# New places for conversions, turns, zeros and one routing chain in a linear-attention and two-MLP kernel

## The chip, the cores and the metric

The kernel runs on one core of one Trainium2 chip. The metric is the device time of one execution in microseconds (us). The engines of a core work from queues of their own, each strictly in order: TensorE (PE; its weight loads are shown as PEld), VectorE (DVE), ScalarE (ACT), GpSimd (POOL) and SyncE (SP), which here issues nearly all DMAs. Matmul results go to PSUM banks and are read from there by VectorE and ScalarE.

## The reference

Three stages, all in float32:

1. Linear attention with decay: 4 batches, 8 heads, 768 steps, head size 48. Per step, `cur = (u*k_t) outer v_t`, `y_t = r_t (state + cur)`, `state = w*state + k_t outer v_t`. The result, regrouped, is `x` of 3072 tokens x 384.
2. An MLP: `h = x @ w_in` (384 x 2048), `g = relu(h)^2`, `x = g @ w_out` (2048 x 384).
3. A mixture of 8 experts with noisy top-2 routing: `noisy = x @ w_gate + log1p(exp(x @ w_noise)) * noise`; the two largest per token are chosen, their softmax gives two weights; each token's output is the weighted sum of `relu(x @ w1[e]) @ w2[e]` (384 x 1024, 1024 x 384) over its two experts.

## The kernel before

All large products are done in a split form: a value is rounded to a shorter float ("high", fp32r) and its remainder kept ("low"), and three matmuls (high x high, high x low, low x high) take the place of one. So each product of 128x128 by 512 columns is three matmuls, and each activation and each weight needs a conversion: ScalarE writes the high part, VectorE (or GpSimd) subtracts to get the low part.

**First part, blocks j = 0 to 5** of 512 tokens. Per block there are 16 steps f. Each step issues mm1(j,f) (nine matmuls into a `ph` bank, of which there are two), gsplit(j,f) (Relu and two Squares on ScalarE, the subtract `gl` on VectorE), then the pieces that were put at slot 2f, then mm2 of two steps earlier (nine matmuls), then the pieces of slot 2f+1. A piece's place is written as a number: `put(8.8, ...)` means slot 8, ordered within it by the fraction. The pieces are the attention of the next block (pre, p_tr, p_a, p_y and so on: CHUNKS), the routing of the block before (ROUTE), and in the last block the preparation of the first experts. The order of a queue is the order in which the code issues; nothing is reordered later.

Attention chunks beyond the eighth read r and k by strided loads on SyncE (`load_next`, L205 to L218) into one buffer each (`rp`), which VectorE turns (L385) and GpSimd scales (L387) for the matmuls of p_a (L414).

**Routing of a block** is a chain: r_row (matmuls with the gate weights), r_soft1 to r_soft3 (softplus, with an Exp and a Ln on ScalarE), r_top1, r_top2, r_sel (small VectorE operations on 128 x 4 x 8), r_rank (three small matmuls on TensorE, L651 to L655, which read `sel`, `pre` and `tot` of r_sel; then VectorE makes the slot numbers `si`), r_w1 and r_w2 (weights, with an Exp), and eight r_send: indirect DMAs on GpSimd that write the tokens' rows to the experts' places in a DRAM buffer `sent`. ROUTE has three tables: for block j=1, for j=2 to 4, and for j=5, which routes block 4.

**Second part, the experts.** An expert e is worked in two units: (e,0), 512 tokens, and (e,1), 308 tokens. A unit fetches its rows (`fetch`: four DMAs of G and two small ones of gt, on SyncE), turns them (`turn`, three per unit: VectorE transposes, ScalarE copies to the high part, VectorE subtracts), goes up (8 steps f with Relu `hh` on ScalarE and `hl` on VectorE) and down. (e,0) goes down in four tiles of 24 matmuls; (e,1) goes down transposed, in three tiles of 24 (`down_t`), each copied out as `yT`, and is turned back in the next unit (`back`). Results are scaled on ScalarE and added to `out` in DRAM by indirect DMAs on GpSimd. The order of units is (0,0), (1,0), (0,1), (1,1), (2,0), (2,1), ..., (6,0), (6,1), (7,1), (7,0).

Expert weights come in eight pieces per expert, four for the first layer (w0) and four for the second (w1): `load_e` on SyncE into three staging buffers `ws` (one in block 5), `conv_e` on ScalarE and VectorE. `conv_next` converts the next piece and issues the load three pieces ahead, which can only start when a staging buffer is free. `put(n, ...)` in a unit gives a place after the Relu of step n (n under 8) or in down step n-8; `fill` holds pieces that are spread evenly over the unit.

`out` is first cleared by zero_out (before: one DMA of 4,800 KB, at slot 2.6 of block 2), and `sent` by eight DMAs of 1,375 KB in block 1.

Of the kernel before, what the change touches and what calls it, by code (L numbers as in the profile page):

```python
# [8 lines left out]
F32 = mybir.dt.float32  # L9
F32R = mybir.dt.float32r  # L10
# [7 lines left out]
P = 128  # L18
# [56 lines left out]


ROUTE_LAST = (0.6, 0.6, 0.8, 1.81, 1.8, 1.81, 2.8, 2.81, 2.82, 3.3, 3.8, 4.8, 5.3, 5.81, 4.8, 5.8, 8.8, 7.82, 10.8,
# [3 lines left out]
FETCH, TOTALS = 13.9, 13.95  # L81
TURN_10 = (8.8, 9.8, 10.8)
TURN_01 = (8.8, 9.8, 10.8)
TURN_11 = (7.3, 7.8, 8.81, 8.82, 8.83, 9.8, 9.81)
TURN = (7.8, 8.8, 8.81)


@with_exitstack
def body(ctx, tc, r, k, v, w, u, w_in, w_out, w_gate, w_noise, noise, w1, w2, out):
    nc = tc.nc  # L90
    B, H, S, D = r.shape
    DM = H * D
    FF = w_in.shape[1]
    E, _, F2 = w1.shape
    NT = B * S
    KD = DM // P
# [3 lines left out]
    NCH = NT // P  # L100
# [19 lines left out]
    def pool(name, side="left", stack=ctx, **kw):  # L120
        return stack.enter_context(tc.tile_pool(name=name, bufs=1, side=side, reuse_waits="tile", **kw))

    consts = pool("consts")
    eb = pool("eb", side="right")
# [4 lines left out]
    C = {}  # L129
# [199 lines left out]
        nc.sync.dma_start(sent[e * CAP:e * CAP + LAST * P, :].rearrange("(q p) x -> p q x", p=P),  # L329
                            C["zero"][:, None, :].to_broadcast([P, LAST, XW]))  # L330

    def zero_out():
        zero = eb.tile([P, DM], F32, name="zero2", tag="s3", bufs=1)
        nc.vector.memset(zero, 0.0)
        nc.sync.dma_start(out.rearrange("(q p) d -> p q d", p=P),
                          zero[:, None, :].to_broadcast([P, NCH + 1, DM]))

    x1h, x1l = {}, {}
    A = {}
# [147 lines left out]
    def mm1(j, f):  # L487
        ph = PH[j, f] = bank("ph", 2)
        qi, fo = divmod(f, NF // NP)
        sl = slice(fo * P, (fo + 1) * P)  # L490
        n = 0
        for d in range(KD):
            for wt, xt in ((wih, x1h), (wih, x1l), (wil, x1h)):
                nc.tensor.matmul(ph, wt[qi][:, d, sl], xt[j][:, d, :], start=(n == 0), stop=(n == 3 * KD - 1))  # L494
                n += 1
# [24 lines left out]
    def finish(j):  # L520
        xo = XO.pop(j)
        X2[j] = eb.tile([P, KD, BLK], F32, name="x2T", tag="s6", bufs=2)
        for d in range(KD):
            (nc.vector.tensor_copy if d == 1 else nc.scalar.copy)(X2[j][:, d, :], xo[:, d, :])
# [165 lines left out]
    W, RW, X, GT, HT, YT, IDX = {}, {}, {}, {}, {}, {}, {}  # L690
# [12 lines left out]
    NW = 4  # L703
# [26 lines left out]
    def tokens(un):  # L730
        a0, a1 = UNITS[un]
        return sum(width(a) for a in range(a0, a1))
# [4 lines left out]
    def fetched(un):  # L737
        return -(-tokens(un) // 32) * 32
# [18 lines left out]
        early.append(nc.sync.dma_start(gt[:, 1, :, None], rows[:, :, XW - 1:]))  # L757
        GT[e, un] = gt

    def turn(e, un, c):  # L760
        pl = pools["f2" if un else "f1"]
        if c == 0:
            X[e, un] = X[e, un], *(pl.tile([P, KD, fetched(un)], F32R, name=f"x{h}{un}") for h in "hl")
        g, xh, xl = X[e, un]
        n = fetched(un) // 32
        xt = pl.tile([P, fetched(un)], F32, name=f"xt{un}")
        nc.vector.transpose(xt.rearrange("p (s i) -> p i s", i=n),
                            g[:, :, 32 * c:32 * c + 32])
        nc.scalar.activation(xh[:, c, :], xt, AF.Copy)
        nc.vector.tensor_tensor(xl[:, c, :], xt, xh[:, c, :].bitcast(F32), op=OP.subtract)  # L770
        if c == KD - 1:
            X[e, un] = xh, xl
            idx = IDX[e, un] = pl.tile([P, UNITS[un][1] - UNITS[un][0]], I32, name=f"id{un}", bufs=2)
            nc.vector.tensor_copy(idx, GT[e, un][:, 1, :])
# [213 lines left out]
    for j in range(NB):  # L988
        slots = [[] for _ in range(2 * NF)]

        def put(n, fn, *args):
            k = int(n)
            slots[k].append((n - k, len(slots[k]), lambda: fn(*args)))

        if j + 1 < NB:
            for i, at_ in enumerate(CHUNKS[min(j, 2)]):
                q = (j + 1) * TPB + i
                todo = [(pre, ()), (p_tr, "r"), (p_tr, "k"), (pre2, ()), (p_kv, ()), (p_a, ()), (p_y, (0,)), (p_y, (1,)),
                        (p_x, ())]
                for n, (fn, args) in zip(at_, todo):  # L1000
                    if q > TPB or fn not in (pre, p_tr):
                        put(n, fn, q, *args)
        if j == 0:
            put(0.6, conv_w3, 2)
            for n in range(AW, 2 * NP):
                for at_, fn in zip(CONV_AT[n - AW], (conv_w1, conv_w2, conv_w3)):
                    put(at_, fn, n)
            put(30.6, load_routing)
        if j == 1:
            for e in range(E):  # L1010
                put(e * 3 // 2 + 3.6, zeros, e)
        if j == 2:
            put(2.6, zero_out)
        if j:
            plan = [(r_row, i) for i in range(TPB)] + [(fn,) for fn in (r_soft1, r_soft2, r_soft3, r_top1, r_top2, r_sel, r_w1, r_rank, r_w2)]
            plan += [(r_send, *divmod(i, 2)) for i in range(2 * TPB)]
            for n, (fn, *args) in zip(ROUTE[0 if j == 1 else 1 if j < NB - 1 else 2], plan):
                put(n, fn, j - 1, *args)
            for i, n in enumerate(RESTS[0 if j == 1 else 1 if j < NB - 1 else 2]):
                put(n, r_rest, j - 1, i)  # L1020
        if j == NB - 1:
            put(4.8, f1_open)
            put(4.8, load_e, 0, 0)
            put(20.8, fetch, 0, 0)
            for n in range(NW):
                put(8.8 + 4 * n, conv_e, 0, n)
                if n + 1 < NW:
                    put(8.8 + 4 * n, load_e, 0, n + 1)
            for c in range(KD):
                put(24.8 + 2 * c, turn, 0, 0, c)  # L1030
            put(30.9, fetch, 1, 0)
        slots = [[p for *_, p in sorted(s, key=lambda x: x[:2])] for s in slots]
        for f in range(NF):
            mm1(j, f)
            gsplit(j, f)
            for p in slots[2 * f]:
                p()
            g = j * NF + f - LAG
            if g >= 0:
                mm2(*divmod(g, NF))  # L1040
                if f == LAG - 1:
                    finish(j - 1)
            for p in slots[2 * f + 1]:
                p()
# [10 lines left out]
    def conv_next(eng=None):  # L1055
        conv_e(*todo.pop(0), eng)
        if len(todo) >= AHEAD:
            load_e(*todo[AHEAD - 1])

    def prepare(e, un):  # L1060
        return [lambda c=c: turn(e, un, c) for c in range(KD)]
# [6 lines left out]
    for e, un in order:  # L1068
        n_up = UNITS[un][1] - UNITS[un][0]
        fill, late = [], {}  # L1070
# [11 lines left out]
        if (e, un) == (0, 0):  # L1082
            plan = [(fn, i) for fn in (r_rest, r_row) for i in range(TPB)] + [(fn,) for fn in (r_soft1, r_soft2, r_soft3, r_top1, r_top2, r_sel, r_table, r_w1, r_rank, r_w2)]
            plan += [(r_send, *divmod(i, 2)) for i in range(2 * TPB)]
            plan = [(n, lambda fn=fn, args=args: fn(NB - 1, *args)) for n, (fn, *args) in zip(ROUTE_LAST, plan)]
            plan += [(n, lambda i=i: conv_next(nc.gpsimd if i < SPLIT_POOL else nc.vector)) for i, n in enumerate(CONV_E)]
            plan += list(zip(TURN_10, prepare(1, 0)))
            plan += [(FETCH, lambda: fetch(0, 1)), (TOTALS, totals)]
            carry = [(n - N0, fn) for n, fn in plan if n >= N0]
            for n, fn in plan:  # L1090
                if n < N0:
                    put(n, fn)
        elif (e, un) == (1, 0):
            for n, fn in carry:
                put(n, fn)
            for n in range(NW):
                put(n + 0.8, conv_next)
            put(NW + 0.8, lambda: fetch(2, 0))
            for n, fn in zip(TURN_01, prepare(0, 1)):
                put(n, fn)  # L1100
            put(TURN_01[-1], lambda: fetch(1, 1))
        elif (e, un) == (0, 1):
            for n, fn in zip(TURN_11, prepare(1, 1) + [conv_next] * NW):
                put(n, fn)
        else:
            if e + 1 < E:
                fill += [lambda: fetch(e + 1, un)] + [conv_next] * NW
            if un == 0 and e + 1 < E:
                fill += prepare(e, 1)
            elif e + 1 < E:  # L1110
                if e + 1 == E - 1:
                    fill += prepare(e + 1, 0)
                for n, fn in zip(TURN, prepare(e + 1, int(e + 1 == E - 1))):
                    put(n, fn)
                if (e, un) == (1, 1):
                    put(TURN[-1], lambda: fetch(3, 0))
            else:
                fill += [lambda: None] * NW
# [65 lines left out]
```

## Time and profile before

| what | value |
|---|---|
| time, three runs | 990.04 us median (989.67 to 991.66) |
| profiled execution | 994.35 us, span of its instructions 992.6 us |
| TensorE busy | 951.0 us (96%), mean granted clock 0.981 |
| VectorE busy | 543.4 us (55%) |
| ScalarE busy | 436.7 us (44%) |
| GpSimd busy | 350.8 us (35%) |
| SyncE's DMA queue (q1) | 91.22 MB, 36.2% of 16 engines' span |
| chain that ended last | PE 76%, DVE 10%, DMA 5%, ACT 3% |

Busy shares are averages over the whole span; matmuls are pipelined and their ends are modelled, so start times tell more than busy time. The granted clock is TensorE's clock as a share of full speed: 1.00 is 2.4 GHz, 0.50 is 1.2 GHz. Times in rows count from the first instruction of the span. In a row of the timeline, "[3.62 <-DMA rp<-in_r]" means that the engine was idle for 3.62 us before it and that this DMA ended the wait. In time, block 2 begins near 220 us, block 5 near 468, the experts at 546, unit (1,1) near 633 and (6,1) near 904.

### The profile page before, as it was taken

The numbers are of one execution on the slowest core, as the hardware profiler recorded it, in microseconds if no ns is written. First come the engines' busy times: TensorE is split into PE (matmuls) and PEld (weight loads), VectorE is DVE, ScalarE is ACT, GpSimd is POOL, SyncE is SP. The second block draws the span as 40 slices with busy tenths as digits, with TensorE's granted clock in tenths as the row PEclk, the third lists the DMA queues.
The fourth block names the chain that finished last, engine by engine and source line by source line (L and its number), as shares of the span: only waits on it lengthen the run. The fifth ranks groups of instructions, "written<-read, shape, count | busy, mean of one in ns | idle before, by whom it ended". The sixth has DMA issues, their size and how long they took to land.

```text
span 992.6 us, 17606 instructions
## 1 busy us (share of the span) xinstructions
PE 951.0 (96%) x6816; PEld 819.2 (83%) x6816; DVE 543.4 (55%) x986; ACT 436.7 (44%) x797; POOL 350.8 (35%) x407
## 2 busy tenths in 40 slices
PE   7898999998999999999998999899999999999995
PEld 6676788777778878877886899889999898989985
DVE  6899956535755673582343663454545454544420
ACT  4666755333344444443653642243434444443320
POOL 5555552553563363454030262022121212222112
PEclk7999999999999999999999999899999999999998
DMA  7645359938333152231033477366645555554112
GB/s 171 158 148 148 115 145 295 256 99 271 74 111 79 45 129 77 60 72 67 1 96 80 132 166 144 86 122 135 123 94 127 102 112 114 114 115 70 20 20 35
DMA packets 193301, 112.35 MB, mean 113 GB/s; under 512 B 131728, under 2 KB 185776, under 8 KB 193200
## 3 DMA queue, kind: packets, MB, share of 16 engines
q1 hardware_dynamic: 181776, 91.22, 36.2%
q0 software_dynamic: 10624, 19.74, 10.9%
q8 instruction: 65, 1.06, 0.4%
q14 instruction: 36, 0.29, 0.1%
q10 hardware_dynamic: 800, 0.02, 0.0%
HBM read 74.83 MB, written 36.12 MB: 112 GB/s over the span
## 4 chain that ended last, share of the span: by engine, by line
PE 76%; DVE 10%; DMA 5%; ACT 3%; issue 2%; SPq 2%; POOL 1%; POOLq 0%; ACTq 0%; DVEq 0%
PE ph L793 18%; PE ph L494 15%; PE xo L517 15%; PE y L844 13%; PE y L876 3%; PE att L432 3%; PE ph L876 2%; PE att L414 2%; PE y L793 2%; PE att L550 2%; DVE t L271 1%; DVE t L270 1%; DVE gl L506 1%; DMA ws<-in_moe_w 1%; DMA stg<-in_moe_w_in 1%
## 5 line engine op out<-in xcount | busy, mean ns | idle before, releaser
L855 POOL DMA_INDIRECT out<-yt,id x56 | 87.2, 1556 | 321.5 <-ACT yt L853 291.9
L506 DVE TENSOR_TENSOR gl<-g,gh 128x512 fp32r<-128x512 f32 x96 | 83.1, 866 | 144.6 <-ACT gh L504 138.6
L830 DVE SCALAR_TENSOR_TENSOR hl<-ph,hh 128x512 fp32r<-128x512 f32 (+1 forms) x112 | 66.6, 598 | 123.2 <-ACT hh L829 123.0
L500 ACT ACTIVATE rt<-ph 128x512 f32<-128x512 f32 x96 | 57.2, 596 | 162.2 <-PE ph L494 151.5
L793 PE MATMUL ph<-xh,w0h 128*128 128x512 f32 (+1 forms) x336 | 120.4, 358 | 4.6 <-ACT yT L880 4.2
L494 PE MATMUL ph<-x1h,wih 128*128 128x512 f32 x288 | 118.3, 411 | 2.4 <-ACT rt L500 1.8
L793 PE MATMUL ph<-xh,w0l 128*128 128x512 f32 (+2 forms) x336 | 117.8, 351 | 0.0
L793 PE MATMUL ph<-xl,w0h 128*128 128x512 f32 (+2 forms) x336 | 117.5, 350 | 0.2 <-DVE xl L770 0.2
L517 PE MATMUL xo<-gh,woh 128*128 128x512 f32 x288 | 115.2, 400 | 2.0 <-ACT gh L504 2.0
L517 PE MATMUL xo<-gh,wol 128*128 128x512 f32 x288 | 112.4, 390 | 0.9 <-POOL wol L284 0.9
L494 PE MATMUL ph<-x1l,wih 128*128 128x512 f32 x288 | 113.2, 393 | 0.1
L494 PE MATMUL ph<-x1h,wil 128*128 128x512 f32 x288 | 113.1, 393 | 0.0
L517 PE MATMUL xo<-gl,woh 128*128 128x512 f32 x288 | 112.6, 391 | 0.5 <-DVE gl L506 0.5
L829 ACT ACTIVATE hh<-ph 128x512 fp32r<-128x512 f32 (+1 forms) x112 | 58.6, 524 | 82.9 <-PE ph L793 77.0
L844 PE MATMUL y<-w1h,hh 128*128 128x384 f32 x256 | 85.7, 335 | 0.0
L844 PE MATMUL y<-w1l,hh 128*128 128x384 f32 x256 | 85.6, 335 | 0.0
L844 PE MATMUL y<-w1h,hl 128*128 128x384 f32 x256 | 85.6, 334 | 0.0
L678 POOL DMA_INDIRECT sent<-row,si x48 | 50.4, 1050 | 70.2 <-DVE si L670 50.6
L793 PEld LDWEIGHTS ph<-xh,w0h 128*128 128x128 f32 x336 | 64.0, 190 | 12.0 <-ACT yT L880 4.4
L793 PEld LDWEIGHTS ph<-xh,w0l 128*128 128x128 f32 x336 | 64.0, 191 | 8.0
L793 PEld LDWEIGHTS ph<-xl,w0h 128*128 128x128 f32 x336 | 64.2, 191 | 7.3 <-DVE xl L770 0.5
L494 PEld LDWEIGHTS ph<-x1h,wih 128*128 128x128 f32 x288 | 54.3, 189 | 19.0 <-ACT rt L500 2.9
(209 smaller groups left out, 2072.6 us busy)
## 6 DMA issues: line engine op xcount, KB each, us to landing
ws<-in_moe_w SPq DMA_DIRECT2D x128, 96.0 KB
ws<-in_moe_w SPq DMA_DIRECT2D x32, 384.0 KB
sent<-zero SPq DMA_DIRECT2D x8, 1375.5 KB
G<-sent SPq DMA_DIRECT2D x36, 192.0 KB
stg<-in_moe_w_in SPq DMA_DIRECT2D x8, 768.0 KB
stg<-in_moe_w_out SPq DMA_DIRECT2D x8, 768.0 KB
out<-zero SPq DMA_DIRECT2D x1, 4800.0 KB
lv<-in_v SPq DMA_DIRECT2D x24, 192.0 KB
```

The lines of the kernel that those rows point to most:

```text
L432: nc.tensor.matmul(pb[32 * n:32 * n + 32, d, :], x, y, skip_group_check=True, **kw)
L494: nc.tensor.matmul(ph, wt[qi][:, d, sl], xt[j][:, d, :], start=(n == 0), stop=(n == 3 * KD - 1))
L500: nc.scalar.activation(rt, ph, AF.Relu)
L506: nc.vector.tensor_tensor(gl, g, gh.bitcast(F32), op=OP.subtract)
L517: nc.tensor.matmul(XO[j][:, d, :], wt[qi][:, fo, sl], gt, start=(f == 0 and n == 0), stop=(f == NF - 1 and n == 2))
L678: st = nc.gpsimd.indirect_dma_start(out=sent, in_=s["row"][:, i, :], in_offset=None, out_offset=bass.IndirectOffsetOnAxis(ap=s["si"][:, i, ...
L793: nc.tensor.matmul(ph[:, c], wt[:, d, sl], xt[:, d, c], start=(m == 0), stop=(m == 3 * KD - 1))
L829: nc.scalar.activation(hh[:, :n], ph, AF.Relu)
L830: nc.vector.scalar_tensor_tensor(hl[:, :n], ph, 0.0, hh[:, :n].bitcast(F32), op0=OP.max, op1=OP.subtract)
L844: nc.tensor.matmul(py, ht[:, sl], wt[:, fo, :], start=(m == 0), stop=(m == 3 * NF2 - 1))
L855: st = nc.gpsimd.indirect_dma_start(out=out, in_=yt, in_offset=None, compute_op=OP.add, out_offset=bass.IndirectOffsetOnAxis(ap=IDX[e, un] ...
L876: nc.tensor.matmul(py[d][:, c], wt[:, fo, sl], ht[:, c], start=(m == 0), stop=(m == 3 * NF2 - 1))
```

## The change

Five groups of edits, all of places in the order of issue; the arithmetic is the same.

- ROUTE's third table: from r_soft3 on, the routing of block 4 comes earlier in block 5 (r_rank from 16.12 to 10.9, the sends from places between 16.16 and 20.68 to places between 12.1 and 16.3).
- `fetch(0,0)` moves from slot 20.8 to 16.7 and `fetch(1,0)` from 30.9 to 27.9. The three turns of (0,0), which came whole at 24.8, 26.8 and 28.8, come in two halves each, the transpose at 21.8, 23.8, 25.8 and the copy and subtract a slot later.
- zero_out goes in five DMAs of 960 KB: three in block 3 (slots 8.7, 14.7, 26.7), two in block 4 (8.7, 14.7). The memset of its source tile comes with the first.
- In unit (0,1), two of the four conversions (first-layer pieces of expert 2) come after the Relus of steps 4 and 5, and the other two after the second and third turn, one each, in place of all four behind the turns. The turns come at 7.8, 8.8, 9.8 in place of 7.3, 7.8, 8.81.
- The three turns of (7,0), which were spread over the up of (6,1), come in the down of (6,0).

```diff
-         (4.22, 4.4, 5.4, 5.47, 5.64, 6.68, 8.57, 8.78, 11.541, 12.732, 12.94, 16.12, 15.66,
-          20.4, 18.2, 16.55, 16.16, 17.28, 17.12, 20.1, 20.68))
+         (4.22, 4.4, 5.4, 5.47, 5.64, 6.68, 7.8, 7.81, 8.7, 9.5, 9.6, 10.9, 10.6,
+          12.1, 12.7, 13.3, 13.9, 14.5, 15.1, 15.7, 16.3))
+CLEAR = {3: (8.7, 14.7, 26.7), 4: (8.7, 14.7)}
+FETCH_00 = 16.7
+TURN_00 = ((21.8, 22.8), (23.8, 24.8), (25.8, 26.8))
...
-TURN_11 = (7.3, 7.8, 8.81, 8.82, 8.83, 9.8, 9.81)
+CONV_2 = (4.8, 5.8, 8.81, 9.81)
+TURN_11 = (7.8, 8.8, 9.8)
 TURN = (7.8, 8.8, 8.81)
+TURN_LAST = (9.8, 10.8, 11.8)
...
-    def zero_out():
-        zero = eb.tile([P, DM], F32, name="zero2", tag="s3", bufs=1)
-        nc.vector.memset(zero, 0.0)
-        nc.sync.dma_start(out.rearrange("(q p) d -> p q d", p=P),
-                          zero[:, None, :].to_broadcast([P, NCH + 1, DM]))
+    def zero_out(i, n):
+        if i == 0:
+            C["zero2"] = eb.tile([P, DM], F32, name="zero2", tag="s3", bufs=1)
+            nc.vector.memset(C["zero2"], 0.0)
+        a, b = i * (NCH + 1) // n, (i + 1) * (NCH + 1) // n
+        nc.sync.dma_start(out[a * P:b * P, :].rearrange("(q p) d -> p q d", p=P),
+                          C["zero2"][:, None, :].to_broadcast([P, b - a, DM]))
...
-    def turn(e, un, c):
+    XT = {}
+
+    def turn(e, un, c, parts="ab"):
         pl = pools["f2" if un else "f1"]
-        if c == 0:
-            X[e, un] = X[e, un], *(pl.tile([P, KD, fetched(un)], F32R, name=f"x{h}{un}") for h in "hl")
+        if "a" in parts:
+            if c == 0:
+                X[e, un] = X[e, un], *(pl.tile([P, KD, fetched(un)], F32R, name=f"x{h}{un}") for h in "hl")
+            n = fetched(un) // 32
+            XT[e, un] = pl.tile([P, fetched(un)], F32, name=f"xt{un}")
+            nc.vector.transpose(XT[e, un].rearrange("p (s i) -> p i s", i=n),
+                                X[e, un][0][:, :, 32 * c:32 * c + 32])
+        if "b" not in parts:
+            return
         g, xh, xl = X[e, un]
-        n = fetched(un) // 32
-        xt = pl.tile([P, fetched(un)], F32, name=f"xt{un}")
-        nc.vector.transpose(xt.rearrange("p (s i) -> p i s", i=n),
-                            g[:, :, 32 * c:32 * c + 32])
+        xt = XT.pop((e, un))
         nc.scalar.activation(xh[:, c, :], xt, AF.Copy)
...
-        if j == 2:
-            put(2.6, zero_out)
+        for i, n in enumerate(CLEAR.get(j, ())):
+            put(n, zero_out, i + sum(len(c) for k, c in CLEAR.items() if k < j), sum(map(len, CLEAR.values())))
...
-            put(20.8, fetch, 0, 0)
+            put(FETCH_00, fetch, 0, 0)
...
-            for c in range(KD):
-                put(24.8 + 2 * c, turn, 0, 0, c)
-            put(30.9, fetch, 1, 0)
+            for c, at_ in enumerate(TURN_00):
+                for n, part in zip(at_, "ab"):
+                    put(n, turn, 0, 0, c, part)
+            put(27.9, fetch, 1, 0)
...
         elif (e, un) == (0, 1):
-            for n, fn in zip(TURN_11, prepare(1, 1) + [conv_next] * NW):
+            for n, fn in zip(CONV_2 + TURN_11, [conv_next] * NW + prepare(1, 1)):
                 put(n, fn)
...
             if un == 0 and e + 1 < E:
                 fill += prepare(e, 1)
+                if e + 1 == E - 1:
+                    for n, fn in zip(TURN_LAST, prepare(e + 1, 0)):
+                        put(n, fn)
             elif e + 1 < E:
-                if e + 1 == E - 1:
-                    fill += prepare(e + 1, 0)
                 for n, fn in zip(TURN, prepare(e + 1, int(e + 1 == E - 1))):
```

## Rows read from the trace of the kernel before

**Rows 1.** Windows: stretch, us; PE, PEld, DVE, ACT, POOL busy; PEclk, DMA, GB/s.
```profile
122.00:209.00 87.00, 87.00 (x685) 69.35 (x677) 50.44 (x108) 38.66 (x68) 44.91 (x52) 1.00 0.77 216
248.93:252.35 3.42, 3.42 (x9) 2.67 (x8) 2.41 (x3) 0.07 (x1) 3.17 (x3) 0.50 0.16 40
531.04:546.24 15.20, 11.67 (x46) 8.21 (x45) 7.24 (x10) 6.80 (x12) 0.00 (x0) 1.00 0.26 53
638.05:644.88 6.83, 6.09 (x24) 6.09 (x25) 1.34 (x2) 1.02 (x3) 0.00 (x0) 0.50 0.54 135
921.36:924.77 3.41, 3.41 (x15) 3.41 (x15) 2.45 (x5) 1.07 (x3) 0.00 (x0) 0.50 0.00 0
```

**Rows 2.** Whom TensorE waited for: us in total, times, longest; the span.
```profile
PE ph L793 <- ACT yT L880: 4.2, 1, 4.2
PE att L414 <- POOL kT L387: 3.1, 1, 3.1
...
PE y L876 <- ACT hh L829: 1.4, 1, 1.4
```

**Rows 3.** Timeline of TensorE in block 5: start, us, engine, line, operation.
```profile
494.11 0.39 PE L517 MATMUL xo<-gh,woh 128*128 128x512 f32 x1
...
496.15 0.39 PE L494 MATMUL ph<-x1h,wih 128*128 128x512 f32 x1
...
531.04 0.39 PE L517 MATMUL xo<-gh,woh 128*128 128x512 f32 x1
...
546.24 0.39 PE L793 MATMUL ph<-xh,w0h 128*128 128x512 f32 x1
```

**Rows 4.** Timeline of TensorE in unit (6,1).
```profile
904.19 0.30 PE L793 MATMUL ph<-xh,w0h 128*128 128x308 f32 x1
...
914.40 0.30 PE L876 MATMUL y<-hh,w1h 128*128 128x308 f32 x1
...
928.95 0.31 PE L793 MATMUL ph<-xh,w0h 128*128 128x308 f32 x1
```

**Rows 5.** Timeline of SyncE's queue: DMA issues of block 2, block 5 and (0,1).
```profile
224.28 8.21 SPq L537 DMA_DIRECT2D noise<-in_moe_noise  x1
...
525.39 2.71 SPq L752 DMA_DIRECT2D G<-sent  x4
...
632.30 1.75 SPq L717 DMA_DIRECT2D ws<-in_moe_w  x4
```

**Rows 6.** Timeline of VectorE in blocks 2 and 5.
```profile
242.80 1.09 DVE L385 STREAM_TRANSPOSE rT<-rp 128x512 f32<-128x512 f32 x1 [3.62 <-DMA rp<-in_r]
...
489.95 0.19 DVE L584 TENSOR_TENSOR d<-d,q 128x32 f32<-128x32 f32 x1
...
492.71 0.18 DVE L589 TENSOR_TENSOR ln<-ln,d 128x32 f32<-128x32 f32 x1
...
496.19 0.69 DVE L506 TENSOR_TENSOR gl<-g,gh 128x512 fp32r<-128x512 f32 x1 [0.23 <-ACT gh L504]
...
497.68 0.19 DVE L563 TENSOR_TENSOR oh<-oh,oh2m 128x32 f32<-128x32 f32 x1
...
500.87 0.18 DVE L613 TENSOR_TENSOR sel<-oh,oh 128x32 bf16<-128x32 f32 x1
...
501.71 0.17 DVE L619 TENSOR_TENSOR tot<-pre,sel 128x8 bf16<-128x8 bf16 x1
...
532.05 1.05 DVE L767 STREAM_TRANSPOSE xt<-G 128x512 f32<-128x512 f32 x1 [6.41 <-DMA G<-sent]
```

**Rows 7.** Timeline of GpSimd in block 5: the first send.
```profile
511.42 1.05 POOL L678 DMA_INDIRECT sent<-row,si  x1 [50.61 <-DVE si L670]
```

**Rows 8.** The chain that ended last, in time: start, us, what.
```profile
521.16 4.15 DMA sent<-row,si
...
633.62 3.82 DMA ws<-in_moe_w
```

**Rows 9.** Timeline of ScalarE in unit (0,1).
```profile
637.60 0.84 ACT L726 ACTIVATE w0h<-ws 128x768 fp32r<-128x768 f32 x1 [4.84 <-DMA ws<-in_moe_w]
```

## The prediction

> **What bounds the kernel now.** Read the list of what TensorE waited for first, then the granted clock in chosen stretches, then the start times of its matmuls around each wait. TensorE is the bound: in most stretches it is busy without a break, for instance all 87 us from 122 to 209 [rows 1]. So the kernel can only become faster where TensorE stands still, and each such place has a price of two parts, the wait and, behind some waits, a stretch at the lower of its two clock levels (0.50, 1.2 GHz), in which the same matmuls take twice as long. Leaving the start of the kernel aside, four places stand out, and the change touches each.
>
> 1. Block 2 (244 us): 3.1 us for kT [rows 2], then 3.42 us at 0.50 [rows 1], of which half is lost: 3.1 + 1.7 = 4.8 us.
> 2. End of block 5: one group of nine matmuls takes 496.15 - 494.11 = 2.04 us [rows 3]. From 531.04 to the first matmul of the experts at 546.24 lie five groups, mm2(12), mm1(15), mm2(13) to mm2(15): 15.2 us where 10.2 would do, so 5.0 us lost.
> 3. From the down of (0,1) into (1,1): 4.2 us for yT [rows 2], then 6.09 us of busy time at 0.50 [rows 1], half of it lost: 7.25 us.
> 4. Unit (6,1): its up, 72 matmuls of 308 columns, takes 914.40 - 904.19 = 10.21 us; its down, again 72 of 308, takes 928.95 - 914.40 = 14.55 us [rows 4], with a wait for hh [rows 2] and a half-clock stretch [rows 1] in it: 4.3 us lost.
>
> Sum of what could go: 4.8 + 5.0 + 7.25 + 4.3 = 21.35 us.
>
> **The change, part by part.**
>
> *Zeros.* One memset stays; SyncE gets four issues more. Before, the 4,800 KB go out in block 2 just ahead of the loads of a chunk: SyncE's next issue takes 8.21 us [rows 5], and VectorE then waits 3.62 us for rp at 242.80 [rows 6]; kT, made behind it, is what TensorE lacks. Without them block 2 is free of its 4.8 us. A piece of 960 KB can hold the loads behind it by 8.21/5 = 1.6 us at least and (242.80 - 224.28)/5 = 3.7 us at most. The first piece of block 3 also keeps SyncE waiting for the memset on VectorE, with the loads of a chunk queued behind; the second pieces of blocks 3 and 4 stand just ahead of such loads; the other two stand where nothing is needed soon. So three times VectorE may find rp late by up to 3.7 us, and gl behind it. A gl has room: mm1(f) ends four groups, 8.2 us, before mm2(f) starts, and the split is three ScalarE operations under 0.84 each [rows 9] and gl's 0.69 [rows 6], so 5 us are free. The nearest row is the stretch from 122 to 209, where eight pieces of 1,375 KB go out between the same sort of loads at 216 GB/s and TensorE is busy throughout [rows 1]. I take 0; the ends are 0 and a full stall of 4.8 us for each of five pieces, 24 us.
>
> The Trainium skill ("DMA: Bandwidth & Descriptors", Queues, rings and completion order) says that on each DMA engine descriptors are consumed in ring order: by that alone a piece still stands in front of every load issued behind it, and the sum would be the 24 us; the trace agrees for the whole transfer (rp 3.62 us late) and not for the pieces of block 1.
>
> *The routing of block 4, fetch and turns in block 5.* Before, the first turn's transpose waited 6.41 us for G and started at 532.05 [rows 6]; ScalarE's copy, queued behind it, held back the Relu of f=13 and everything after: the 5.0 us. The rank step moves from slot 16.12 to 10.9, 5.2 slots of 2.04 us = 10.7 us. Now its inputs are late. Soft2 ends on VectorE at 489.95 + 0.19 = 490.14. What stood between, soft3, top1, top2, one subtract of a weight conversion and one gl, ran from 492.71 to 497.87 with 0.23 idle, 4.93 us; sel to tot ran from 500.87 to 501.88, 1.01 us [rows 6]. In the new order these run back to back: tot is there at 490.14 + 4.93 + 1.01 = 496.1. The rank matmuls now stand after mm1(5), in front of mm2(3), which started at 494.11 [rows 3]. TensorE waits 2.0 us. Ends: 0, and 2.0 + 1.7 = 3.7 if the clock falls behind it; below 0 is excluded, since nothing gets shorter there. ScalarE too stands before the Exp of w1, ahead of the Relu of f=5, by about 2 us; that Relu has three groups, 6.1 us, until mm1(7) needs its bank. I take 2.0 without a fall, since the waits in the 15.2 us at the end of block 5 brought none [rows 1].
>
> The sends then start 10.7 - 2.0 = 8.7 us earlier than 511.42 [rows 7], the last one lands at 521.16 + 4.15 - 8.7 = 516.6 [rows 8], and G at 532.05 - 8.7 = 523.3.
>
> What is late next is on SyncE: fetch(0,0), now at slot 16.7, stands in front of the load of weight piece (0,3) at 16.8. SyncE stays there until 516.6, issues G in 2.71 us [rows 5] and two small ones in at most 1.4 (each under a G issue), and starts the load at 520.7. The same kind of load took 633.62 + 3.82 - 632.30 = 5.1 us [rows 5, 8]: 525.8. ScalarE's conversion (slot 20.8) waits for it, takes 0.84 [rows 9], and the Relu of f=11 behind it ends at about 527.2. mm1(13) needs that bank at 531.04 - 3 x 2.04 + 2.0 = 526.9: 0.3 us of wait. Ends: 0, and with the 6.7 us that G took from 525.39 to 532.05, 1.9 us. I take 0.3, from the same kind of transfer. VectorE, in order, stands at that conversion's subtract until 526.6; subtract (0.69 x 768/512 = 1.0), the first transpose (1.05, slot 21.8, G long there) and the gl of f=11 (0.69) end at 529.4 [rows 6], and mm2(11), from 526.9 + 0.3 + 2.04 = 529.2, reads gl in its second matmul: nothing more. ScalarE's copy of a turn comes a slot after its transpose and so no longer holds a Relu. Then the turns follow in the gaps that ScalarE has in each f (three operations under 0.84 in 4.1 us), and mm2(15) waits for nothing: the 5.0 us go. fetch(1,0) at 27.9 waits for the last transpose with nothing queued behind it but the experts' next loads: 0.
>
> *Conversions in (0,1).* Before, four conversions ran together behind the turns; the fourth waited 4.84 us for weights [rows 9] whose load only the first could release (issue at 632.30 [rows 5], landed at 637.4 [rows 8]), and the yT copy that TensorE needed stood behind it. Now the first follows the Relu of f=4. It is sooner by three groups of the up (10.21/8 = 1.28 us each at most, by [rows 4]) and at least one of the three down tiles (3.4), some 7 us; the load lands by about 630, and ScalarE comes to the fourth conversion only after the second down tile. The two in the up cost 0.84 on ScalarE and 0.69 x 768/512 = 1.0 us on VectorE each [rows 6, 9]; they push hl of f=6 back by about 1 us, and the down reads f=0 to 5 first. I take 0 for them and 7.25 gained; if the down did wait for hl it would be about 1 us. The price if the fourth load is still late is all of the 7.25.
>
> *Turns of (7,0).* A turn is 1.05 (transpose) + under 0.84 (copy) + 0.69 (subtract, by gl) = 2.6 us [rows 6, 9]. Three leave the up of (6,1), where Relus stand behind them, for the down of (6,0), 96 matmuls with one eviction per 24, longer than the 10.21 us of 72 [rows 4]. They fit beside the three turns of (6,1) already there. Cost 0, at most 2.6 if the last is late; gain 4.3.
>
> Sum: -21.35 + 2.0 + 0.3 = -19.05. The profiled execution, 994.35 us (span 992.6 and 1.75 around it), would become 975.3. It stands 4.3 us over the median of 990.04; the stalls belong to the order of the work, so I take the same difference there: **971.0 us**.
>
> **Rivals.**
> A, the rank matmuls don't hold TensorE (VectorE packs its small operations closer than before): 990.04 - 21.35 + 0.3 = 969.0. Against it: they depend on one another.
> B, the new order of block 5 costs more: the load behind the fetch lands late (1.9) and both new waits pull the clock down (2 x 1.7): 971.0 + 1.6 + 3.4 = 976.0. For it: the half-clock stretch in (6,1), behind a wait of 1.4 us for hh [rows 2]. Against it: none at the end of block 5.
> C, one edit doesn't do what it says: the fourth load of (0,1) or the turns in (6,1) are late as before: 971.0 + 7.25 = 978.3, or 971.0 + 4.3 = 975.3. For it: other loads and fetches share SyncE.
> D, slower: every piece of zeros delays a chunk's loads as the whole did, since SyncE is one queue and TensorE pays 4.8 us each time: 971.0 + 24.0 = 995.0. It decides from four pieces on (19.05/4.8). For it: three of the five stand ahead of such loads. Against it: block 1. The Trainium skill's ring order ("DMA: Bandwidth & Descriptors", Queues, rings and completion order) would be its ground.
>
> **Chances.** Forecast 0.57 (its own range 968 to 974), A 0.08, B 0.15, C 0.13, D 0.07; in 0.02 of that last only three or four pieces stall. The range 967 to 979 holds the forecast, A, B and C. About 0.2% (2 us) is what a measurement tells from no change: faster 0.93, same 0.02, slower 0.05.
>
> **What would show it.** No wait for kT near 244 and none with L385 ahead of it in blocks 3 and 4; a wait of about 2 us before the first rank matmul (L651's step) in block 5; the Relus of f=13 to 15 on time and mm2(12) to the experts in 10.2 us; ScalarE's fourth w0h conversion of block 5 waiting for ws; no yT wait at (1,1) and no half clock there; (6,1) with equal up and down. The forecast is wrong if the rank wait is missing, if ScalarE's wait for ws in block 5 exceeds some 8 us, or if new waits for kT or am appear in blocks 3 and 4.

## The result, and the profile after

The changed kernel takes 971.87 us median (970.9 to 972.28, four runs) against 990.71 us of the kernel before beside it: a ratio of 0.9812, 95% interval 0.9801 to 0.9824, 18.84 us less. Predicted were 971.0 us, 19.05 less than the median then known. The profiled execution went from 994.35 to 972.28 us, 22.07 us; the fourth step below takes up the 3.2 us between the two differences.

First, whom TensorE waited for from 130 to 970 us (us in total, times, longest). This is the whole list. The waits of [rows 2] for kT, yT and hh are gone, and so are those of the end of block 5, the largest of which is the first line below, from the list of the kernel before. One new wait is there, for the rank's inputs; the wait for xl at the start of (2,0) was there before.

```profile
PE xo L517 <- ACT gh L504: 2.0, 2, 1.2
```

```profile
PE att L658 <- DVE pre L622: 0.9, 1, 0.9
PE att L660 <- DVE pre L624: 0.4, 1, 0.4
PE ph L806 <- DVE xl L783: 0.2, 1, 0.2
```

Windows of the changed kernel, columns as in [rows 1]: the stretch of the zeros of `sent`, block 2, the end of block 5, the start of (1,1), and (6,1). TensorE is busy throughout at 1.00; none of the three half-clock stretches of [rows 1] is left.

```profile
122.00:209.00 87.00, 87.00 (x688) 69.29 (x677) 50.75 (x109) 39.03 (x69) 44.84 (x52) 1.00 0.77 216
240.00:260.00 20.00, 20.00 (x205) 15.96 (x204) 15.05 (x42) 9.51 (x17) 9.39 (x9) 1.00 0.32 70
520.00:560.00 40.00, 40.00 (x194) 34.19 (x192) 22.42 (x56) 24.16 (x42) 7.36 (x5) 1.00 0.37 100
622.00:645.00 23.00, 23.00 (x169) 22.94 (x168) 12.63 (x20) 10.55 (x21) 4.69 (x6) 1.00 0.63 146
899.00:909.00 10.00, 10.00 (x75) 10.00 (x75) 3.81 (x8) 2.35 (x6) 0.00 (x0) 1.00 0.00 0
```

TensorE's timeline in block 5: mm1(5), the rank matmuls, mm2(3), then mm2(12) and the first matmul of the experts. mm1(5) ends at 485.59 + 2.04 = 487.63 and mm2(3) starts at 489.53, 1.9 us later (the two waits, 0.92 and 0.42 us, and the rank matmuls themselves); in [rows 3] it followed at once. From mm2(12) to the experts it is 10.20 us, where [rows 3] have 15.20.

```profile
485.59 0.39 PE L501 MATMUL ph<-x1h,wih 128*128 128x512 f32 x1
...
488.70 0.19 PE L658 MATMUL att<-sel,mask 128*128 128x32 bf16 x1 [0.92 <-DVE pre L622]
489.31 0.18 PE L660 MATMUL att<-pre,ones 128*128 128x32 bf16 x1 [0.42 <-DVE pre L624]
...
489.53 0.48 PE L524 MATMUL xo<-gh,woh 128*128 128x512 f32 x1
...
526.35 0.39 PE L524 MATMUL xo<-gh,woh 128*128 128x512 f32 x1
...
536.55 0.39 PE L806 MATMUL ph<-xh,w0h 128*128 128x512 f32 x1
```

VectorE of the changed kernel: two transposes of block 3 that wait for rp behind a piece of zeros; the end of soft2 and tot in block 5 (483.66 to 489.46, 5.8 us, where 5.94 were reckoned); and the subtract of the fourth weight conversion with the first turn's transpose right behind it.

```profile
328.84 1.09 DVE L392 STREAM_TRANSPOSE rT<-rp 128x512 f32<-128x512 f32 x1 [1.88 <-DMA rp<-in_r]
...
348.35 1.09 DVE L392 STREAM_TRANSPOSE rT<-rp 128x512 f32<-128x512 f32 x1 [4.11 <-DMA rp<-in_r]
...
483.47 0.19 DVE L591 TENSOR_TENSOR d<-d,q 128x32 f32<-128x32 f32 x1
...
489.30 0.16 DVE L626 TENSOR_TENSOR tot<-pre,sel 128x8 bf16<-128x8 bf16 x1
...
517.95 0.96 DVE L734 TENSOR_TENSOR w0l<-ws,w0h 128x768 fp32r<-128x768 f32 x1 [5.14 <-ACT w0h L733]
518.82 1.08 DVE L776 STREAM_TRANSPOSE xt<-G 128x512 f32<-128x512 f32 x1
```

GpSimd's first send starts at 495.81 (511.42 in [rows 7]); SyncE then issues G and, behind it, the load of weight piece (0,3); ScalarE waits for that load in block 5 and no longer for the fourth one of (0,1), which is converted at 622.36 (637.60 with 4.84 us of wait in [rows 9]).

```profile
508.46 2.71 SPq L759 DMA_DIRECT2D G<-sent  x4
...
512.51 1.83 SPq L724 DMA_DIRECT2D ws<-in_moe_w  x4
```

```profile
517.07 0.85 ACT L733 ACTIVATE w0h<-ws 128x768 fp32r<-128x768 f32 x1 [4.99 <-DMA ws<-in_moe_w]
...
622.36 0.83 ACT L733 ACTIVATE w0h<-ws 128x768 fp32r<-128x768 f32 x1
```

TensorE in (6,1): up 896.86 - 886.73 = 10.13 us, down 906.95 - 896.86 = 10.09 us; in [rows 4] 10.21 and 14.55.

```profile
886.73 0.30 PE L806 MATMUL ph<-xh,w0h 128*128 128x308 f32 x1
...
896.86 0.30 PE L889 MATMUL y<-hh,w1h 128*128 128x308 f32 x1
...
906.95 0.30 PE L806 MATMUL ph<-xh,w0h 128*128 128x308 f32 x1
```

### The profile page after: what moved, and what is told of

The parts are those of the page before. It is cut to its first block, busy times and chain, and to the rows that moved or that the text cites. A ratio compares the mean times of both kernels' runs of the same rounds, so it can differ in the third digit from the quotient of the medians.

```text
span 970.6 us, 17617 instructions
## 1 busy us (share of the span) xinstructions
PE 941.2 (97%) x6816; PEld 812.9 (84%) x6816; DVE 543.2 (56%) x986; ACT 437.3 (45%) x797; POOL 351.3 (36%) x407
## 4 chain that ended last, share of the span: by engine, by line
PE 84%; DVE 8%; DMA 2%; ACT 2%; issue 1%; SPq 1%; POOL 0%; POOLq 0%; ACTq 0%; DVEq 0%
PE ph L806 19%; PE xo L524 17%; PE ph L501 17%; PE y L857 13%; PE y L889 4%; PE att L439 4%; PE ph L889 2%; PE att L421 2%; PE att L557 2%; PE y L806 2%; DVE t L276 1%; DVE t L275 1%; DMA stg<-in_moe_w_in 1%; DVE t L274 1%; DVE gl L513 1%
## 5 line engine op out<-in xcount | busy, mean ns | idle before, releaser
L513 DVE TENSOR_TENSOR gl<-g,gh 128x512 fp32r<-128x512 f32 x96 | 80.7, 841 | 145.2 <-ACT gh L511 141.9
```

The lines of the kernel that those rows point to most:

```text
L513: nc.vector.tensor_tensor(gl, g, gh.bitcast(F32), op=OP.subtract)
```

## The experiments

Twelve kernels ran: the changed kernel once more (after_again) and eleven with a few of its places altered. Each was timed against the kernel before on its own chip; the ratio says more than the median, since the kernel before took 990.7 to 992.6 us on these chips.

| kernel | median us | before us | ratio | 95% interval |
|---|---|---|---|---|
| undo_zeros | 977.91 | 992.06 | 0.9859 | 0.9843 to 0.9876 |
| undo_block5 | 975.04 | 992.06 | 0.9835 | 0.9821 to 0.9849 |
| undo_conv | 980.20 | 992.06 | 0.9879 | 0.9860 to 0.9899 |
| undo_turns | 976.43 | 992.06 | 0.9846 | 0.9833 to 0.9860 |
| after_again | 975.69 | 992.61 | 0.9826 | 0.9812 to 0.9840 |
| rank_later | 974.14 | 992.61 | 0.9808 | 0.9793 to 0.9822 |
| load_first | 975.02 | 992.61 | 0.9814 | 0.9799 to 0.9830 |
| zeros_split_b2 | 978.89 | 992.61 | 0.9864 | 0.9845 to 0.9883 |
| zeros_whole_b4 | 984.56 | 990.76 | 0.9941 | 0.9927 to 0.9955 |
| conv_one | 973.02 | 990.76 | 0.9820 | 0.9806 to 0.9834 |
| route_late | 983.65 | 990.76 | 0.9924 | 0.9910 to 0.9938 |
| best | 969.12 | 990.76 | 0.9791 | 0.9773 to 0.9808 |

**Each part undone.** Four kernels take back one part each.

```diff
-CLEAR = {3: (8.7, 14.7, 26.7), 4: (8.7, 14.7)}
+CLEAR = {2: (2.6,)}
```

> The changed kernel with the output's zeros back as one DMA of 4,800 KB at slot 2.6 of block 2, all else as changed. Theory (the whole transfer makes rp late and TensorE lacks kT): the wait for kT near 244 us and a half-clock stretch behind it come back, 4.8 us, so about 976.7 us. Rival (the wait came from something else that the change moved too): no change, 971.9 us.

The wait is back, 3.0 us, with 3.41 us at 0.50 behind it:

```profile
PE att L421 <- POOL kT L394: 3.0, 1, 3.0
```

```profile
246.89:250.30 3.41, 3.41 (x15) 2.60 (x14) 2.45 (x5) 0.23 (x1) 2.73 (x3) 0.50 0.36 89
```

```diff
-FETCH_00 = 16.7
-TURN_00 = ((21.8, 22.8), (23.8, 24.8), (25.8, 26.8))
+FETCH_00 = 20.8
+TURN_00 = ((24.8, 24.8), (26.8, 26.8), (28.8, 28.8))
...
```

> The changed kernel with block 5 as before: the routing of block 4, fetch(0,0), fetch(1,0) and the whole turns of (0,0) at their old places. Theory: the 5.0 us at the end of block 5 come back and the 1.9 us wait of the rank matmuls goes, 3.1 us more, so about 975.0 us. Rival (the earlier loads of the experts that follow have a worth of their own): over 976 us.

ROUTE's third table and fetch(1,0) at 30.9 go back with them. The waits at the end of block 5 are back (gh 2.0 us, rt 0.6, gl 0.4) and the rank's is gone: 975.04 us.

```diff
-CONV_2 = (4.8, 5.8, 8.81, 9.81)
-TURN_11 = (7.8, 8.8, 9.8)
+CONV_2 = (8.82, 8.83, 9.8, 9.81)
+TURN_11 = (7.3, 7.8, 8.81)
```

> The changed kernel with the four conversions and three turns of (0,1) as before. Theory: the wait for yT of 4.2 us and the half clock behind it come back, 7.25 us, so about 979.1 us. Rival (with the rest moved, the weights land in time anyway): 971.9 us.

ScalarE's fourth conversion waits 5.70 us for its load and TensorE 5.0 us for yT; 6.82 us at 0.50 begin towards the end of that wait:

```profile
628.97 0.84 ACT L733 ACTIVATE w0h<-ws 128x768 fp32r<-128x768 f32 x1 [5.70 <-DMA ws<-in_moe_w]
```

```profile
PE ph L806 <- ACT yT L893: 5.0, 1, 5.0
```

```profile
628.82:635.64 6.82, 5.47 (x21) 5.47 (x22) 1.35 (x2) 1.48 (x3) 0.00 (x0) 0.50 0.49 127
```

```diff
-                    for n, fn in zip(TURN_LAST, prepare(e + 1, 0)):
-                        put(n, fn)
...
+                if e + 1 == E - 1:
+                    fill += prepare(e + 1, 0)
```

> The changed kernel with the turns of (7,0) back in the up of (6,1). Theory: the waits for hh in (6,1) and the half clock behind them come back, 4.3 us, so about 976.2 us. Rival (the fall of the clock behind waits this short is not there in every run): 2.5 us or less, 974.4 us or under.

The waits in (6,1), 1.4 us for hh and 0.8 for hl, and the fall of the clock behind them are back:

```profile
PE y L889 <- ACT hh L842: 1.4, 1, 1.4
PE y L889 <- DVE hl L843: 0.8, 2, 0.4
```

```profile
902.62:906.03 3.41, 3.41 (x16) 3.41 (x15) 2.09 (x6) 1.40 (x3) 0.00 (x0) 0.50 0.00 0
```

In each case the wait named in the prediction returned. Three of the four profiles also have a wait of 0.6 to 0.8 us for xh at the start of (2,0), which the first profile of the changed kernel lacks; after_again has it with nothing altered, so it is not the work of these edits.

The medians give the sizes only roughly, since the changed kernel did not run beside these four. Against its 0.9812 the ratios are worse by 0.47, 0.23, 0.67 and 0.34 points, 1.71 together, while the whole change is worth 1.88. Against the 0.9826 of after_again they are 0.14 smaller each, 1.15 together, while the change is then worth 1.74. The traces settle it: compare the start times of the same TensorE matmuls ahead of and behind each place with those of the changed kernel. The four cost 4.7, 2.7, 7.7 and 4.8 us there, 19.9 together. The kernel before, read in the same way, loses 4.8, 3.2, 7.1 and 4.5 us at these places, 19.6 together. So the parts add up, and none needs another.

**The changed kernel again, the rank matmuls, and the load behind the fetch.**

> The changed kernel once more, beside the three variants of this call, so that their differences are taken against it on one chip: 0.981 of the kernel before. Nothing is left open by it but the size of the differences.

0.9826 on this chip, the two intervals overlapping. Its profiled execution, 978.75 us, is 6.5 us over the first one's without a change in the order. At two places (L439 at 210 us, L465 at 365 us) TensorE stood for nothing that the trace names; by the start times each cost 1.7 us. At the start of (2,0) it waited 1.0 us for xh, and here the clock fell behind the wait; together this cost 3.0 us.

```profile
PE ph L806 <- ACT xh L782: 1.0, 1, 1.0
...
PE att L465 <- issue: 0.9, 2, 0.5
PE att L439 <- issue: 0.8, 2, 0.5
```

```profile
652.10:655.51 3.41, 3.41 (x10) 2.72 (x11) 0.93 (x2) 1.17 (x2) 0.94 (x1) 0.50 1.04 223
```

```diff
-          (4.22, 4.4, 5.4, 5.47, 5.64, 6.68, 7.8, 7.81, 8.7, 9.5, 9.6, 10.9, 10.6,
+          (4.22, 4.4, 5.4, 5.47, 5.64, 6.68, 7.8, 7.81, 8.7, 9.5, 9.6, 11.5, 10.6,
```

> The changed kernel with r_rank at slot 11.5 in place of 10.9, so that the three rank matmuls stand behind mm2(3) in place of in front of it. Theory (TensorE stands 1.8 us because tot of r_sel comes late, and nothing else is late): mm2(3) fills the time, the wait goes, 1.8 us less than the changed kernel; the sends start at the same time, since r_w2 and the gl of f=5 stand before the rank's VectorE part anyway. Rival (the Exp of r_w1 on ScalarE, which waits for the same chain, holds the Relu of f=5 and with it mm1(7)): the wait moves there, no change.

TensorE has no wait at all from 400 to 550 us; by the start times 1.8 us are gained there, and the median is 1.55 us under after_again's. Nothing took the wait's place: the Relu of f=5 had the room that the prediction gave it, and the first send starts 10.2 us after mm1(5) begins, as in after_again. The intervals of the ratios overlap, so the size rests on the traces and not on the times alone.

```diff
-FETCH_00 = 16.7
+FETCH_00 = 16.9
```

> The changed kernel with fetch(0,0) at slot 16.9 in place of 16.7, so that the load of weight piece (0,3) goes out ahead of the fetch on SyncE. Theory (ScalarE's 5.0 us wait for that load is hidden, since the Relu of f=11 has as much room): the wait goes and the time stays, within 0.5 us of the changed kernel. Rival (the wait costs TensorE something that the start times do not show): 1 us or more faster.

ScalarE's fourth conversion no longer waits for its DMA, and the time is the same: from mm1(5) to the experts TensorE takes just as long as in the changed kernel. The median is 0.7 us under after_again's, a little more than the 0.5 expected but well inside the intervals. The 4.99 us were hidden.

```diff
-         (4.22, 4.4, 5.4, 5.47, 5.64, 6.68, 7.8, 7.81, 8.7, 9.5, 9.6, 10.9, 10.6,
-          12.1, 12.7, 13.3, 13.9, 14.5, 15.1, 15.7, 16.3))
+         (4.22, 4.4, 5.4, 5.47, 5.64, 6.68, 8.57, 8.78, 11.541, 12.732, 12.94, 16.12, 15.66,
+          16.2, 16.25, 16.3, 16.35, 16.4, 16.45, 16.5, 16.55))
```

> The changed kernel with the routing of block 4 late in block 5 again (r_rank at 16.12, the sends right behind it), while fetch(0,0) stays at 16.7, ahead of the load of weight piece (0,3). Theory (SyncE stands at the fetch until the sends have landed, the load behind it is late by as much, and ScalarE's conversion holds the Relu of f=11): TensorE waits some 10 us before mm1(13) and the clock falls behind it; the rank wait goes: about 10 us over the changed kernel, near 985 us on a chip where that takes 975.7. Rival (ScalarE and the load have room enough): the rank wait goes and nothing else, 1.8 us under it.

With late sends SyncE issues G at 519.09 and the load at 523.14; ScalarE waits 16.95 us for it, TensorE 10.0 us for the Relu, and 10.24 us at 0.50 begin in that wait. The time is 1.0 to 1.1 points over the changed kernel, some 10 to 11 us, as expected. So the queue order that cost nothing with early sends is among the most expensive edits here with late ones: the pipeline of steps hides about 7 us of ScalarE's wait (16.95 less 10.0), no more.

```profile
527.99 0.84 ACT L733 ACTIVATE w0h<-ws 128x768 fp32r<-128x768 f32 x1 [16.95 <-DMA ws<-in_moe_w]
```

```profile
PE ph L501 <- ACT rt L507: 10.0, 1, 10.0
```

```profile
523.67:533.91 10.24, 4.54 (x11) 3.58 (x12) 4.80 (x6) 5.30 (x10) 0.00 (x0) 0.50 0.34 52
```

**Zeros: place or size.**

```diff
-CLEAR = {3: (8.7, 14.7, 26.7), 4: (8.7, 14.7)}
+CLEAR = {2: (2.6, 2.61, 2.62, 2.63, 2.64)}
```

> The changed kernel with the five pieces of zeros issued one behind the other at the old place, slots 2.6 to 2.64 of block 2. Theory (the place counts: the bytes stand ahead of the loads of a chunk): as with the whole transfer, 4.9 us over the changed kernel. Rival (the size of one DMA counts: pieces let other loads in between): no more than 1 us over it.

The wait for kT is back, 3.1 us, with 3.41 us at 0.50 from 248.33. By the start times it costs 4.8 us, as with one DMA (4.7); the median is 3.2 us over after_again's. Cutting alone helps nothing.

```diff
-CLEAR = {3: (8.7, 14.7, 26.7), 4: (8.7, 14.7)}
+CLEAR = {4: (8.7,)}
```

> The changed kernel with the zeros as one DMA of 4,800 KB again, but at slot 8.7 of block 4, where the first piece of that block stood. Theory (the place counts, not the size): what stands behind it there, the loads of a chunk some 9 us later, has slack, so within 1 us of the changed kernel, with a wait of VectorE for rp but none of TensorE. Rival (16 us of zeros are late for somebody anywhere): TensorE lacks kT in block 4, some 4 us more.

Both theories missed. It is the slowest of the twelve, 1.2 to 1.3 points over the changed kernel (12.6 us by the start times). VectorE stood 13.36 us at the transpose of rp, and behind that the `am` copy that frees a PSUM bank, for which TensorE waited 10.2 us:

```profile
421.84 1.08 DVE L392 STREAM_TRANSPOSE rT<-rp 128x512 f32<-128x512 f32 x1 [13.36 <-DMA rp<-in_r]
```

```profile
PE att L465 <- DVE am L425: 10.2, 1, 10.2
```

```profile
418.21:428.45 10.24, 4.91 (x91) 4.16 (x92) 6.37 (x13) 0.23 (x1) 4.33 (x5) 0.50 0.33 70
```

The place was not the quiet one that I took it for: with the memset beside it, SyncE could issue the zeros only at 402.56 (396.08 for the piece of the changed kernel, whose memset had long been done), right ahead of the loads of a chunk. So this run does not part place from memset. An estimate: without these 6.5 us VectorE would still have stood some 6.9 us and TensorE some 3.7, near the size that the rival gave. Together with zeros_split_b2 it shows that both count: the bytes that stand ahead of a chunk's loads at one time, and how soon these are wanted. 960 KB made VectorE wait 1.88 and 4.11 us, under the 5 us that gl has; 4,800 KB made it 13.36. The zeros also hold SyncE: its issue of the noise load took 8.21 us behind them in block 2 of the kernel before [rows 5], and 0.57 us at 218.59 in the changed kernel, where none stand ahead.

**Conversions: release or crowding.**

```diff
-CONV_2 = (4.8, 5.8, 8.81, 9.81)
+CONV_2 = (4.8, 8.81, 9.81, 9.82)
```

> The changed kernel with only the first conversion of (0,1) early (4.8), the other three at 8.81, 9.81 and 9.82. Theory (the early release of the staging buffer, so that the fourth piece is loaded in time, is what counts): the fourth conversion does not wait for its DMA, and no wait for yT over 1 us comes back: within 1 us of the changed kernel. Rival (four conversions so near the yT copies are too much work there): the yT wait of some 4 us and the half clock come back, 7 us more.

0.9820, inside both intervals of the changed kernel, and no yT wait in the trace. The fourth conversion does not wait for its load. So the early release of one staging buffer is enough; the three turns kept their new places here, and no run took these back by themselves.

**The fastest version.**

```diff
-          (4.22, 4.4, 5.4, 5.47, 5.64, 6.68, 7.8, 7.81, 8.7, 9.5, 9.6, 10.9, 10.6,
+          (4.22, 4.4, 5.4, 5.47, 5.64, 6.68, 7.8, 7.81, 8.7, 9.5, 9.6, 11.5, 10.6,
...
-FETCH_00 = 16.7
+FETCH_00 = 16.9
...
-                for n, fn in zip(TURN, prepare(e + 1, int(e + 1 == E - 1))):
+                for n, fn in zip((7.3, 7.5, 8.8) if e == 1 else TURN, prepare(e + 1, int(e + 1 == E - 1))):
```

> The changed kernel with r_rank at 11.5, fetch(0,0) behind the load (16.9), and in unit (1,1) two of the three turns of (2,0) ahead of the last weight conversion, which waits for its DMA. Theory: no rank wait (1.8 us) and no wait for xl at the start of (2,0) (0.6 us, in some runs with a fall of the clock up to 3 us): some 2.5 us under the changed kernel, 0.978 of the kernel before. Rival (the two turns delay the relus or the loads behind them): no better than with r_rank moved alone, 0.981.

969.12 us, ratio 0.9791 (0.9773 to 0.9808): below after_again's whole interval, but overlapping those of the first comparison and of rank_later. Beside it on the same chip conv_one, close to the changed kernel, took 973.02 us. In the trace of best TensorE waits for nothing between 130 and 970 us, the start of (2,0) included, where rank_later still waited 1.0 us for xh. So the traces speak against the rival, no better than with r_rank moved alone; the times do not part the two.

## Why the prediction was right, step by step

1. *Zeros, 4.8 us.* Right, with its ground: undone, 3.0 us of wait and 3.41 us at 0.50 return. VectorE was to find rp late three times by up to 3.7 us; it did twice, by 1.88 and 4.11, the second above the bound. TensorE paid nothing, as said. The rival D had the right mechanism and the wrong size for these pieces: zeros_whole_b4 shows it with the whole transfer, 10.2 us of wait and a fall of the clock. The ring order that the Trainium skill ("DMA: Bandwidth & Descriptors", Queues, rings and completion order) names agrees with these traces: VectorE waited 1.88, 4.11 and 13.36 us behind zeros. What decides is how much stands ahead, which that sentence leaves open.
2. *End of block 5, 5.0 us gained, 2.0 and 0.3 lost.* The gain: 15.20 to 10.20 us. The rank wait: 1.9 us measured, and rank_later takes it away by one group of matmuls. Rival A is out. The load behind the fetch cost nothing: it was issued 4.05 us after G, as reckoned (4.1), and landed in 4.5 us where 5.1 were taken. The Relu of f=11 ended at 518.40, 1.8 us before mm1(13) started at 520.23; the sum had it 0.3 us late, so it took the margin as thinner than it was. route_late shows where the margin ends: 10.0 us of wait from the same order. No clock fell (rival B).
3. *Conversions of (0,1), 7.25 us, and turns of (7,0), 4.3 us.* The same matmul, the first of (6,1), starts 904.19 - 886.73 = 17.46 us earlier and the first of the experts 546.24 - 536.55 = 9.69: 7.8 us were won between, about 0.6 of it at the start of (2,0), which the sum did not have. (6,1) gave 4.5. Rival C is out.
4. *From the profile to the median.* Here the prediction was right partly by luck. It took a profiled execution of 975.3 us, and the median 4.3 us under it as in the kernel before. The profile came out at 972.28, 3.0 us lower, and lay only 0.4 us over its median: two errors of 3.0 and 3.9 us that nearly cancel. In the profiles 22.07 us were won where the sum had 19.05. Of the 3.0 us more, 1.6 are a pause of TensorE near 210 us in the profile of the kernel before (L432; 0.7 us of it stand in its list of waits as "issue"), 0.6 are the start of (2,0), 0.3 the load that cost nothing, and the rest small differences in the other terms. The medians moved by 18.84. Pauses at the same matmuls (L439 in the changed kernel) stand in all four profiles taken on after_again's chip and in none of the other nine of the changed kernel and its variants. What makes them, and what part of them is in the medians, stays open.

## What to carry to other kernels

Where TensorE is busy nearly always, list its waits one by one, price each as wait plus half of any half-clock stretch behind it, and check for each edit what stands behind it on every in-order queue that it is moved past. Adding an engine's small operations end to end, from the last thing they wait for, gave the new wait to 0.1 us (2.0 reckoned, 1.9 measured). A bulk transfer with no deadline should be cut and spread, so that what stands ahead of a load at any time is less than that load's slack. Cutting it alone did nothing here; what an earlier memset is worth by itself no run shows.

## What the runs showed of the hardware

TensorE's clock fell to 0.50 at single waits of 3.0 us and more, and behind waits of 1.4 and twice 0.4 us close together in (6,1) (undo_turns). It did not fall behind the rank matmuls' 0.92 and 0.42 us, nor behind the several waits of the end of block 5. At the start of (2,0), waits of 1.0 us for xh and 0.2 for xl brought 3.41 us at 0.50 in after_again and route_late, and none in rank_later and conv_one. So the length of a wait alone does not tell whether the clock falls. In the two runs with a wait of some 10 us the stretch at 0.50 began in the wait and lasted 10.24 us. And TensorE can pause for nothing that the trace names, 1.5 to 1.8 us by the start times: at 210 us in all four profiles of one chip and in that of the kernel before, at 365 us in three of the four, and in none of the other nine.
